# Moving transposes and small gradients in the backward pass of a convolution and joint kernel

## The chip, the cores and the metric

The kernel runs on one core of a Trainium2 chip. The metric is the device time of one execution in microseconds (us). A core has five engines with queues of their own: TensorE (PE, matmuls and transposes into PSUM; PEld is its weight load), VectorE (DVE), ScalarE (ACT), GpSimd (POOL) and SyncE (SP), which issues DMAs here. Engines wait for each other by semaphores, and each works through its queue in order.

## The reference

`x` is (2, 16000, 256), the weights `w1` and `w2` are (3, 256, 256), `g` is (2, 8, 256), and `w_f`, `w_g`, `w_o` are (256, 256), all bf16. The outputs are the forward result and the gradients of all seven inputs.

```python
def conv_half(h, w):                       # 3 taps, padded by 1, then every second row
    hp = jnp.pad(h, ((0,0),(1,1),(0,0)))
    f = sum(jnp.einsum("btc,cd->btd", hp[:, i:i+h.shape[1], :], w[i]) for i in range(3))
    return gelu(f)[:, ::2, :]

f = conv_half(conv_half(x, w1), w2)                        # (2, 4000, 256)
fe, ge = f @ w_f, g @ w_g
j = jnp.tanh(fe[:, :, None, :] + ge[:, None, :, :])        # (2, 4000, 8, 256)
out = jnp.einsum("btud,dv->btuv", j, w_o)
# vjp with grad_out (2, 4000, 8, 256): gradients of x, w1, w2, g, w_f, w_g, w_o
```

## The kernel before, in words

The 4000 rows of each of the two batches are cut into eight chunks of 512 rows (the last has 416), 16 chunks in all, numbered n = 0 to 15. Features lie on the partitions, in two halves of 128; rows lie on the free dimension.

For each chunk the kernel computes, under these names:

- `conv_units`: the first convolution (L246), `HT` after gelu and its derivative `G1`; `conv2_units`: the second one (L279), `FT` and `G2`; `fe_units`: FE = FT times w_f (L302). The gelu is a chain of instructions (`gelu`, L197 and L199): copies of PSUM to `g_x` (L282 in `conv2_units`), the square `g_sq` on ScalarE, `g_s` on VectorE, a sigmoid on ScalarE, and the product (HT or FT) on VectorE; the derivative follows (L199).
- `joint_units`, four times a chunk, each for two of the eight values of u: `gj` computes the square `JSQ` of the tanh (L523), the product of w_o and the transposed gradient (L529), and `NGZ` = (JSQ - 1) times it (L531); `ngfe_acc` sums NGZ over u on GpSimd (L550); `o_block` computes the output (L623, copied out by L625); `gwo` adds to the gradient of w_o in one PSUM tile that lives to the end (L672); `ahead` issues the tanhs of the next pair (L312).
- the backward pass of the chunk before: `d1_units` (GF, L336 and L338), `d5_units` (GH, L366 and L369), `gwf_units` (gradient of w_f, L406), `gw2_units` (rows of HT and GF by transposes on PE, L380, copied by ScalarE, L382, then three groups of w2 products, L437), `e_units`. The last one transposes GH in two groups (L380, copied to `rows` by VectorE, L382), and then goes through the blocks of 128 rows: `gx_block` computes the gradient of x in two halves (L478, copied by L481) and stores it by a DMA on the GpSimd queue (L490); `gw1` computes a group of w1 products (L500), one after each of the first three blocks.

The products of w1, w2 and w_f of a chunk are added to sums in SBUF by `flush` (L320 for the first chunk, L322 after it): ACC1, ACC2, ACCF.

The order of the work: chunk n's joint units are the main line. `weave` takes one piece of the fill (the first convolution of chunk n+1, the backward pass of chunk n-1, the second convolution and FE of n+1) after a piece of the main line, 0.85 pieces on average. The fill's order is written out by hand in the list `parts` (L771 to L787): near its end come the last pieces of w2, `conv2_units`, six pieces of `e_units` (two transposes, four of gx and w1), `fe_units`, and the rest of `e_units`. VectorE's pieces of gelu wait in a queue that `pump` empties. A scheduler then assigns buffers and writes each engine's queue, so that the queues are fixed before the kernel runs. PSUM has one tile for the gradient of w_o and seven that all other results take in turn. JSQ has two buffers, NGZ three, GX two.

After the last chunk comes a tail (L813 to L860): the remaining pieces of w_o's gradient, then `d1`, `d5`, `gwf`, `gw2` and `e` of chunk 15 one after the other, then copies of the sums to bf16 and their stores on SP (L821 to L833), and at the end the gradients of g and w_g: NGGE is the sum over the chunks (L836), and for each batch there are two products with w_g (L845), two transposes (L851), a copy (L853) and two products with g (L855), and at last a copy and a store (L859, L860).

Of the kernel before, what the change touches and what calls it, by code (L numbers as in the profile page):

```python
# [32 lines left out]
def kernel(  # L33
# [279 lines left out]
                                 bias=GE[:, b, mt, u:u + 1], scale=1.0)  # L313


    first_flush = {"1": True, "2": True, "F": True}

    def flush(key, acc, ps):
        if first_flush[key]:
            nc.vector.tensor_copy(out=acc, in_=ps)  # L320
        else:
            nc.vector.tensor_tensor(out=acc, in0=acc, in1=ps, op=ALU.add)  # L322

    def d1_units(n):
        b, ci, c0, W = geom(n)
# [58 lines left out]
    def gwf_units(n):  # L384
        b, ci, c0, W = geom(n)
        st = S[n]
        HT, GF, FT, NG = st["HT"], st["GF"], st["FT"], st["NGFE"]
        bl = blocks(W)
        FN = []
        for k in range(0, len(bl), 2):  # L390
            t = rowp.tile([P, 8, P], BF16, name="rows")
            srcs, dsts = [], []
            for j, (o, M) in enumerate(bl[k:k + 2]):
                for kt in range(KT):
                    srcs.append((FT[:, kt, o:o + M], 4 * j + kt, M))
# [13 lines left out]
        flush("F", ACCF[:], ps[:])  # L409
        first_flush["F"] = False  # L410
        yield

    def gw2_units(n):
        b, ci, c0, W = geom(n)
        st = S[n]
        HT, GF, FT, NG = st["HT"], st["GF"], st["FT"], st["NGFE"]
        bl = blocks(W)
        HG = []
        for (o, M) in bl:
            t = rowp.tile([P, 8, P], BF16, name="rows")  # L420
            srcs = []
            j = 0
            for (par, off) in ((0, 2), (1, 2), (1, 1)):
                for kt in range(KT):
                    srcs.append((HT[:, par, kt, off + o:off + o + M], j, M))
                    j += 1
            for kt in range(KT):
                srcs.append((GF[:, kt, 2 + o:2 + o + M], j, M))
                j += 1
            transposes(srcs, [(t[:M], M, 0, 8)], nc.scalar.copy)  # L430
            HG.append(t)
            yield
        for i, place in ((1, 0), (2, 2), (0, 4)):
            ps = ps_f32()
# [5 lines left out]
            flush("2", ACC2[:, i, :], ps[:])  # L440
            yield
        first_flush["2"] = False
    def e_units(n):
        b, ci, c0, W = geom(n)
        st = S[n]
# [48 lines left out]
        def gw1(i):  # L494
            ps = ps_f32()
            for k, (o, M) in enumerate(bl):
                t, j = GR[k]
                for dt in range(KT):
                    for par in range(2):
                        nc.tensor.matmul(ps[:, dt * D:(dt + 1) * D],  # L500
                                         lhsT=st["X5", o][:M, i + 2 * par, dt * P:(dt + 1) * P],
                                         rhs=t[:M, j + 2 * par:j + 2 * par + 2, :].rearrange("p k d -> p (k d)"),
                                         start=(k == 0 and dt == 0 and par == 0),
                                         stop=(k == len(bl) - 1 and dt == KT - 1 and par == 1))
            flush("1", ACC1[:, i, :], ps[:])
# [6 lines left out]
        first_flush["1"] = False  # L512


    n_gwo = [0]
# [246 lines left out]
    for n in range(G):  # L762
# [3 lines left out]
        if back:  # L766
            for (o, M) in blocks(window(n - 1)[1] - window(n - 1)[0]):
# [16 lines left out]
        if fwd:  # L784
# [5 lines left out]
        for up in range(U // 2):  # L790
# [17 lines left out]
            if up == U // 2 - 1:  # L808
                for _ in fill:
                    pump(2)  # L810
                pump(len(later) + len(lazy))
                lazy_on[0] = False
    n = G - 1  # L813
    gwo_rest(*prev_gwo[0], 0)
    for (o, M) in blocks(window(n)[1] - window(n)[0]):
        load_x5(n, o, M)
    for _ in chain(d1_units(n), d5_units(n), gwf_units(n), gw2_units(n), e_units(n)):
        pass


    for i in range(KK):  # L821
        t_ = gel3.tile([P, 512], BF16, name="g_sq", tag="g_sq")
        nc.scalar.copy(out=t_[:], in_=ACC1[:, i, :])
        nc.sync.dma_start(out=out_2[i].rearrange("(dt p) n -> p dt n", p=P), in_=t_[:].rearrange("p (k n) -> p k n", k=KT))
        t_ = gel3.tile([P, 512], BF16, name="g_s", tag="g_s")
        nc.vector.tensor_copy(out=t_[:], in_=ACC2[:, i, :])
        nc.sync.dma_start(out=out_3[i].rearrange("(dt p) n -> p dt n", p=P), in_=t_[:].rearrange("p (k n) -> p k n", k=KT))
    t_ = gel.tile([P, 512], BF16, name="g_x", tag="g_x")
    nc.vector.tensor_scalar(out=t_[:], in0=ACCF[:], scalar1=-1.0, scalar2=None, op0=ALU.mult)
    nc.sync.dma_start(out=out_5.rearrange("(dt p) n -> p dt n", p=P), in_=t_[:].rearrange("p (k n) -> p k n", k=KT))  # L830
    t_ = gel.tile([P, 512], BF16, name="g_x", tag="g_x")
    nc.scalar.copy(out=t_[:], in_=GWO_ps[:].rearrange("p k v -> p (k v)"))
    nc.sync.dma_start(out=out_7.rearrange("(dt p) n -> p dt n", p=P), in_=t_[:].rearrange("p (k n) -> p k n", k=KT))  # L833

    NGGE = const.tile([P, B, KT, U], FP32, name="NGGE")
    nc.vector.tensor_reduce(out=NGGE[:].rearrange("p b k u -> p (b k u)"),  # L836
                            in_=NGGEc[:].rearrange("p b k u c -> p (b k u) c"),
                            axis=mybir.AxisListType.X, op=ALU.add)
    NGGEb = const.tile([P, B, KT, U], BF16, name="NGGEb")
    nc.vector.tensor_copy(out=NGGEb[:], in_=NGGE[:])  # L840
    GWG_ps = ps_f32()
    for b in range(B):
        gg = ps_f32()
        for kt in range(KT):
            nc.tensor.matmul(gg[:U, 0:D], lhsT=NGGEb[:, b, kt, :], rhs=WGT[:, kt, :], start=(kt == 0), stop=(kt == KT - 1))  # L845
        gg_sb = gxp.tile([U, D], BF16, name="gg_sb")
        nc.scalar.activation(out=gg_sb[:], in_=gg[:U, 0:D], func=ACT.Copy, scale=-1.0)
        nc.sync.dma_start(out=out_4[b], in_=gg_sb[:])
        tr = ps_bf()
        for kt in range(KT):  # L850
            nc.tensor.transpose(out=tr[:U, kt, :], in_=NGGEb[:, b, kt, :], identity=ident[:])  # L851
        ngR = gxp.tile([U, KT, P], BF16, name="ngR")
        nc.vector.tensor_copy(out=ngR[:], in_=tr[:U, 0:KT, :])  # L853
        for dt in range(KT):
            nc.tensor.matmul(GWG_ps[:, dt * D:(dt + 1) * D], lhsT=GR8[:, b, dt * P:(dt + 1) * P],  # L855
                             rhs=ngR[:].rearrange("u kt p -> u (kt p)"),
                             start=(b == 0 and dt == 0), stop=(b == B - 1 and dt == KT - 1))
    t_ = gel3.tile([P, 512], BF16, name="g_sq", tag="g_sq")
    nc.scalar.activation(out=t_[:], in_=GWG_ps[:], func=ACT.Copy, scale=-1.0)  # L859
    nc.sync.dma_start(out=out_6.rearrange("(dt p) n -> p dt n", p=P), in_=t_[:].rearrange("p (k n) -> p k n", k=KT))  # L860


# [1 line left out]
_INS = ['x', 'w1', 'w2', 'g', 'w_f', 'w_g', 'w_o', 'grad_out']  # L864
_OUTS = [((2, 4000, 8, 256), 'bfloat16'), ((2, 16000, 256), 'bfloat16'), ((3, 256, 256), 'bfloat16'), ((3, 256, 256), 'bfloat16'), ((2, 8, 256), 'bfloat16'), ((256, 256), 'bfloat16'), ((256, 256), 'bfloat16'), ((256, 256), 'bfloat16')]
# [25 lines left out]
```

## Time and profile before

| | |
|---|---|
| three runs, median (lowest to highest) | 867.71 us (865.87 to 876.6) |
| the profiled execution | 865.23 us, of which the span is 863.5 us |
| granted clock of TensorE | 0.998 of full speed |
| period of a full chunk (L302 at 573.08 and 625.47 us) | 52.4 us |
| busy share of PE in 100 us to 800 us | 97.6 to 98.8% in each 100 us |
| last 31.5 us | PE busy 25.4 us |

A line of the profile's time line has the start and the duration in us, the engine, the line of the program, the operation, what it writes and reads, and how many instructions were merged; in brackets, the idle time of the engine before it and what ended it. Matmuls overlap, so the time from one start to the next says more than a duration. A line of the list of waits has the engine and what waited, what it waited for, the us in total, how often, and the longest.

### The profile page before, as it was taken

Reading aid. Unit: us, or ns where it says so; the run is one execution under the profiler, and the core shown is the slowest. Engines: PE = TensorE matmul, PEld = TensorE weight load, DVE = VectorE, ACT = ScalarE, POOL = GpSimd, SP = SyncE. Lnnn points to the kernel's source line nnn. Section 1 sums busy time; section 2 is a strip of 40 time slices with the busy share of each in tenths; the row PEclk is TensorE's granted clock in tenths of the full one; section 3 lists DMA queues with packets and bytes.
Section 4 is the critical chain, followed back from the end, with each engine's and each line's share of the span. In section 5 each row is a group of like instructions: output and inputs, shape, how many; then the busy total and the mean of one; then the engine's idle time right before and its main releaser. Section 6 shows DMA issues by size and latency. Waiting matters only on the chain.

```text
span 863.5 us, 17775 instructions
## 1 busy us (share of the span) xinstructions
PE 830.8 (96%) x6648; PEld 598.9 (69%) x6648; DVE 603.8 (70%) x1194; ACT 685.7 (79%) x1067; POOL 410.6 (48%) x457
## 2 busy tenths in 40 slices
PE   8878999999999999999999999999999999999997
PEld 4455776767777677777766677776766867777875
DVE  4797949669495784949578495875949579495553
ACT  4889896986969869696996969788696986969534
POOL 1264553544544544555454455453554544455651
PEclk9999999999999999999999999999999999999999
DMA  9998999999999999999899999999999999999942
GB/s 187 211 215 195 189 250 224 224 243 193 258 206 227 226 217 233 212 227 219 211 203 214 234 215 240 227 210 250 177 263 236 205 211 219 219 243 219 215 140 91
DMA packets 382455, 185.66 MB, mean 215 GB/s; under 512 B 330160, under 2 KB 366280, under 8 KB 382368
## 3 DMA queue, kind: packets, MB, share of 16 engines
q1 hardware_dynamic: 362400, 114.35, 76.4%
q0 software_dynamic: 19968, 70.18, 27.9%
q8 instruction: 52, 0.85, 0.4%
q14 instruction: 35, 0.29, 0.1%
HBM read 54.43 MB, written 50.34 MB: 121 GB/s over the span
## 4 chain that ended last, share of the span: by engine, by line
PE 51%; DVE 30%; ACT 13%; issue 3%; DMA 2%; POOL 0%; ACTq 0%; POOLq 0%; DVEq 0%
PE ps L500 7%; PE ps L246 7%; PE GWO_ps L672 7%; PE ps L529 7%; PE ps L478 7%; PE ps L623 6%; DVE NGZ L531 6%; DVE G L199 5%; DVE g_sq L199 5%; DVE g_s L197 5%; DVE GH L369 3%; ACT JSQ L523 3%; ACT JT L312 3%; PE pst L380 3%; PE ps L366 3%
## 5 line engine op out<-in xcount | busy, mean ns | idle before, releaser
L550 POOL TENSOR_TENSOR ACCN<-ACCN,NGZ 128x1024 f32<-128x1024 f32 (+1 forms) x80 | 170.4, 2130 | 126.5 <-DVE NGZ L531 124.0
L531 DVE SCALAR_TENSOR_TENSOR NGZ<-JSQ,ps 128x512 bf16<-128x512 bf16 (+1 forms) x256 | 163.4, 669 | 83.5 <-ACT GX L481 47.7
L523 ACT ACTIVATE JSQ<-JT 128x1024 bf16<-128x1024 bf16 (+1 forms) x128 | 135.3, 1060 | 86.6 <-DVE NGZ L531 86.6
L312 ACT ACTIVATE JT<-FE,GE 128x512 bf16<-128x512 f32 (+1 forms) x256 | 171.0, 736 | 0.1
L625 ACT CAST OUT<-ps 128x512 bf16<-128x512 f32 x248 | 147.7, 614 | 3.8 <-PE ps L623 3.3
L623 PE MATMUL ps<-WO,JT 128*128 128x256 bf16 x992 | 148.1, 272 | 0.9 <-DVE NGZ L531 0.5
L529 PE MATMUL ps<-GOT,WOT 128*128 128x512 bf16 (+1 forms) x512 | 138.4, 374 | 1.7 <-DVE JR L382 1.1
L672 PE MATMUL GWO_ps<-GO,JR 128*128 128x256 bf16 x992 | 139.7, 273 | 0.0
L197 DVE SCALAR_TENSOR_TENSOR g_s<-g_sq,g_x 128x1024 bf16<-128x1024 bf16 (+1 forms) x45 | 74.6, 1657 | 57.1 <-ACT g_sq L197 57.1
L623 PEld LDWEIGHTS <-JT 128*128 128x128 bf16 x992 | 94.4, 98 | 24.9 <-issue 1.4
L672 PEld LDWEIGHTS <-JR 128*128 128x128 bf16 x992 | 95.1, 98 | 18.2 <-issue 1.1
L322 DVE TENSOR_TENSOR ACC<-ACC,ps 128x512 f32<-128x512 f32 x90 | 59.4, 682 | 66.6 <-PE ps L500 62.0
L478 PE MATMUL ps<-W1T,GH 128*128 128x256 bf16 (+2 forms) x768 | 104.2, 273 | 0.0
L500 PE MATMUL ps<-rows,X 128*128 128x256 bf16 (+2 forms) x768 | 94.2, 272 | 8.2 <-DVE rows L382 8.2
L246 PE MATMUL ps<-XC,W 128*128 128x512 bf16 (+1 forms) x384 | 91.1, 374 | 2.5 <-DMA XC<-in_x_dram 2.1
L500 PEld LDWEIGHTS <-X 128*128 128x128 bf16 (+2 forms) x768 | 74.5, 98 | 23.1 <-issue 11.5
L652 POOL DMA_DIRECT2D out_dram<-OUT x64 | 49.6, 775 | 85.2 <-ACT OUT L625 82.8
L481 ACT CAST GX<-ps 128x512 bf16<-128x512 f32 (+2 forms) x128 | 74.4, 592 | 15.0 <-PE ps L478 7.8
L478 PEld LDWEIGHTS <-GH 128*128 128x128 bf16 (+2 forms) x768 | 75.0, 99 | 15.6 <-issue 1.7
L529 PEld LDWEIGHTS <-WOT 128*128 128x128 bf16 x512 | 49.1, 98 | 43.9 <-issue 2.6
L490 POOL DMA_DIRECT2D out_dram<-GX x64 | 35.9, 560 | 87.3 <-ACT GX L481 81.0
L382 ACT COPY rows<-pst 128x1024 bf16<-128x1024 bf16 x64 | 63.0, 1018 | 9.6 <-PE pst L380 9.5
(139 smaller groups left out, 1264.5 us busy)
## 6 DMA issues: line engine op xcount, KB each, us to landing
GO<-in_grad_out_dram SPq DMA_DIRECT2D x56, 512.0 KB, 5.3
out_dram<-OUT POOLq DMA_DIRECT2D x56, 512.0 KB, 5.6
X<-in_x_dram POOLq DMA_DIRECT2D x58, 320.0 KB, 8.0
out_dram<-GX POOLq DMA_DIRECT2D x58, 256.0 KB, 4.1
JR<-JT SPq DMA_TRANSPOSE x240, 5.1
GO<-in_grad_out_dram SPq DMA_DIRECT2D x8, 384.0 KB, 4.1
out_dram<-OUT POOLq DMA_DIRECT2D x8, 384.0 KB, 4.7
GOT<-in_grad_out_dram SPq DMA_TRANSPOSE x128, 4.6
```

Of the source, the lines that this page charges most:

```text
L197: later.popleft()()
L246: nc.tensor.matmul(ps[:, :W], lhsT=W1[:, i, kt, mt * P:(mt + 1) * P], rhs=st["X", c][:, kt, 16 + sh:16 + sh + W], start=(k == 0), stop=(k ...
L312: nc.scalar.activation(out=JT[:, mt, :W], in_=S[n]["FE"][:, mt, :W], func=ACT.Tanh, bias=GE[:, b, mt, u:u + 1], scale=1.0)
L478: nc.tensor.matmul(ps[:Mx, cj * D:(cj + 1) * D], lhsT=GH[:, par, kt, j:j + Mx], rhs=W1T[:, i, kt, :], start=(k == 0), stop=(k == last))
L500: nc.tensor.matmul(ps[:, dt * D:(dt + 1) * D], lhsT=st["X5", o][:M, i + 2 * par, dt * P:(dt + 1) * P], rhs=t[:M, j + 2 * par:j + 2 * par + ...
L523: nc.scalar.activation(out=JSQ[:, :, :W], in_=JT[:, :, :W], func=ACT.Square)
L529: nc.tensor.matmul(ps[:, :W], lhsT=WOT[:, kt, mt * P:(mt + 1) * P], rhs=GOT[:, kt, :W], start=(kt == 0), stop=(kt == KT - 1))
L531: nc.vector.scalar_tensor_tensor(out=NGZ[:, mt, :W], in0=JSQ[:, mt, :W], scalar=1.0, in1=ps[:, :W], op0=ALU.subtract, op1=ALU.mult, accum_ ...
L550: nc.gpsimd.tensor_tensor(out=out, in0=in0, in1=st["NGZ", u][:, :, :W], op=ALU.add)
L623: nc.tensor.matmul(ps[:M, j * V:(j + 1) * V], lhsT=st["JT", u][:, kt, o:o + M], rhs=WO[:, kt, :], start=(kt == 0), stop=(kt == KT - 1))
L625: nc.scalar.copy(out=OUT[:M, k, :], in_=ps[:M, :])
L672: nc.tensor.matmul(GWO_ps[:, dt, :], lhsT=JR[:M, k, j, dt, :], rhs=GO[:M, k, j * V:(j + 1) * V], start=(n_gwo[0] == 0), stop=(n_gwo[0] == ...
```

## The change

It has four parts. GH's two groups of transposes, the first two pieces of `e_units`, move in the list of the fill from behind `conv2_units` to before the first and before the second group of w2 products, and the pieces of `e_units` between `conv2_units` and `fe_units` are four instead of six. In the last chunk `flush` writes the sum of ACC and PSUM directly to a bf16 tile and stores it. The gradients of w_o, g and w_g become a generator, `small_gradients`, whose pieces stand between those of the last chunk's backward pass. And in the last chunk `e_units` runs the three groups of w1 products first, each followed by a block of gx, and the blocks from the last to the first.

```diff
-    def flush(key, acc, ps):
-        if first_flush[key]:
+    def flush(n, key, i, ps):
+        acc = {"1": ACC1, "2": ACC2}[key][:, i, :] if key != "F" else ACCF[:]
+        if n == G - 1:
+            t = gel3.tile([P, 512], BF16, name="g_sq", tag="g_sq")
+            if key == "F":
+                nc.vector.scalar_tensor_tensor(out=t[:], in0=acc, scalar=-1.0, in1=ps, op0=ALU.mult, op1=ALU.subtract)
+            else:
+                nc.vector.tensor_tensor(out=t[:], in0=acc, in1=ps, op=ALU.add)
+            out = out_5 if key == "F" else {"1": out_2, "2": out_3}[key][i]
+            store_small(out, t)
+        elif n == 0:
             nc.vector.tensor_copy(out=acc, in_=ps)
         else:
             nc.vector.tensor_tensor(out=acc, in0=acc, in1=ps, op=ALU.add)
+    def store_small(out, t):
+        nc.sync.dma_start(out=out.rearrange("(dt p) n -> p dt n", p=P), in_=t[:].rearrange("p (k n) -> p k n", k=KT))
...
+        if n == G - 1:
+            for i in range(KK):
+                gw1(i)
+                yield from gx_block(*bl[-1 - i])
+            yield from gx_block(*bl[0])
+            return
         for k, (o, M) in enumerate(bl):
             yield from gx_block(o, M)
...
-                      islice(d5, 1), islice(gw2, 1), d5, islice(gw2, nhg - 2), gwf, gw2]
+                      islice(d5, 1), islice(gw2, 1), d5, islice(gw2, nhg - 2), gwf, islice(e, 1), islice(gw2, 1),
+                      islice(e, 1), gw2]
...
-            parts.append(islice(e, 6))
+            parts.append(islice(e, 4))
...
+    def small_gradients():
+        t_ = gel.tile([P, 512], BF16, name="g_x", tag="g_x")
+        nc.scalar.copy(out=t_[:], in_=GWO_ps[:].rearrange("p k v -> p (k v)"))
+        store_small(out_7, t_)
...
+        yield
+        GWG_ps = ps_f32()
+        for b in range(B):
+            gg = ps_f32()
+            for kt in range(KT):
+                nc.tensor.matmul(gg[:U, 0:D], lhsT=NGGEb[:, b, kt, :], rhs=WGT[:, kt, :],
+                                 start=(kt == 0), stop=(kt == KT - 1))
...
+            nc.vector.tensor_copy(out=ngR[:], in_=tr[:U, 0:KT, :])
+            yield
+            for dt in range(KT):
+                nc.tensor.matmul(GWG_ps[:, dt * D:(dt + 1) * D], lhsT=GR8[:, b, dt * P:(dt + 1) * P],
...
+        store_small(out_6, t_)
+        yield
...
-    for _ in chain(d1_units(n), d5_units(n), gwf_units(n), gw2_units(n), e_units(n)):
+    small = small_gradients()
+    for _ in chain(d1_units(n), islice(small, 1), d5_units(n), islice(small, 1), gwf_units(n), islice(small, 1),
+                   gw2_units(n), small, e_units(n)):
         pass
-    for i in range(KK):
-        t_ = gel3.tile([P, 512], BF16, name="g_sq", tag="g_sq")
-        nc.scalar.copy(out=t_[:], in_=ACC1[:, i, :])
...
```

More of the change, by code (lines that the diff above doesn't have):

```diff
@@ L313, in tanh @@
                                  bias=GE[:, b, mt, u:u + 1], scale=1.0)
-    first_flush = {"1": True, "2": True, "F": True}
-    def flush(key, acc, ps):
-        if first_flush[key]:
+    def flush(n, key, i, ps):
[9 more added lines that the diff above has]
+        elif n == 0:
             nc.vector.tensor_copy(out=acc, in_=ps)
@@ L408, in gwf_units @@
                                  start=(k == 0 and dt == 0), stop=(k == len(FN) - 1 and dt == KT - 1))
-        flush("F", ACCF[:], ps[:])
-        first_flush["F"] = False
+        flush(n, "F", 0, ps[:])
         yield
@@ L439, in gw2_units @@
                                      start=(k == 0 and dt == 0), stop=(k == len(bl) - 1 and dt == KT - 1))
-            flush("2", ACC2[:, i, :], ps[:])
+            flush(n, "2", i, ps[:])
             yield
-        first_flush["2"] = False
     def e_units(n):
@@ L504, in gw1 @@
                                          stop=(k == len(bl) - 1 and dt == KT - 1 and par == 1))
-            flush("1", ACC1[:, i, :], ps[:])
+            flush(n, "1", i, ps[:])
+        if n == G - 1:
[4 more added lines that the diff above has]
+            return
         for k, (o, M) in enumerate(bl):
@@ L511, in e_units @@
                 yield
-        first_flush["1"] = False
     n_gwo = [0]
@@ L812 @@
                 lazy_on[0] = False
+    def small_gradients():
+        t_ = gel.tile([P, 512], BF16, name="g_x", tag="g_x")
+        nc.scalar.copy(out=t_[:], in_=GWO_ps[:].rearrange("p k v -> p (k v)"))
+        store_small(out_7, t_)
+        NGGE = const.tile([P, B, KT, U], FP32, name="NGGE")
+        nc.vector.tensor_reduce(out=NGGE[:].rearrange("p b k u -> p (b k u)"),
+                                in_=NGGEc[:].rearrange("p b k u c -> p (b k u) c"),
+                                axis=mybir.AxisListType.X, op=ALU.add)
+        NGGEb = const.tile([P, B, KT, U], BF16, name="NGGEb")
+        nc.vector.tensor_copy(out=NGGEb[:], in_=NGGE[:])
+        yield
[5 more added lines that the diff above has]
+                                 start=(kt == 0), stop=(kt == KT - 1))
+            gg_sb = gxp.tile([U, D], BF16, name="gg_sb")
+            nc.scalar.activation(out=gg_sb[:], in_=gg[:U, 0:D], func=ACT.Copy, scale=-1.0)
+            nc.sync.dma_start(out=out_4[b], in_=gg_sb[:])
+            tr = ps_bf()
+            for kt in range(KT):
+                nc.tensor.transpose(out=tr[:U, kt, :], in_=NGGEb[:, b, kt, :], identity=ident[:])
+            ngR = gxp.tile([U, KT, P], BF16, name="ngR")
+            nc.vector.tensor_copy(out=ngR[:], in_=tr[:U, 0:KT, :])
+            yield
+            for dt in range(KT):
+                nc.tensor.matmul(GWG_ps[:, dt * D:(dt + 1) * D], lhsT=GR8[:, b, dt * P:(dt + 1) * P],
+                                 rhs=ngR[:].rearrange("u kt p -> u (kt p)"),
+                                 start=(b == 0 and dt == 0), stop=(b == B - 1 and dt == KT - 1))
+        t_ = gel.tile([P, 512], BF16, name="g_x", tag="g_x")
+        nc.scalar.activation(out=t_[:], in_=GWG_ps[:], func=ACT.Copy, scale=-1.0)
+        store_small(out_6, t_)
+        yield
     n = G - 1
@@ L816 @@
         load_x5(n, o, M)
-    for _ in chain(d1_units(n), d5_units(n), gwf_units(n), gw2_units(n), e_units(n)):
-        pass
-    for i in range(KK):
-        t_ = gel3.tile([P, 512], BF16, name="g_sq", tag="g_sq")
-        nc.scalar.copy(out=t_[:], in_=ACC1[:, i, :])
[L824 to L857, printed above, removed]
@@ L858 @@
-    t_ = gel3.tile([P, 512], BF16, name="g_sq", tag="g_sq")
-    nc.scalar.activation(out=t_[:], in_=GWG_ps[:], func=ACT.Copy, scale=-1.0)
-    nc.sync.dma_start(out=out_6.rearrange("(dt p) n -> p dt n", p=P), in_=t_[:].rearrange("p (k n) -> p k n", k=KT))
+    small = small_gradients()
+    for _ in chain(d1_units(n), islice(small, 1), d5_units(n), islice(small, 1), gwf_units(n), islice(small, 1),
+                   gw2_units(n), small, e_units(n)):
+        pass
 _INS = ['x', 'w1', 'w2', 'g', 'w_f', 'w_g', 'w_o', 'grad_out']
```

## The prediction

> **What bounds the kernel now.** I read the page's busy shares first, then the list of what TensorE (PE) waited for, then the time lines of the four engines around one place, then the end of the chain.
>
> ```profile
> PE 830.8 (96%) x6648; PEld 598.9 (69%) x6648; DVE 603.8 (70%) x1194; ACT 685.7 (79%) x1067; POOL 410.6 (48%) x457
> ```
> PE is the bound: 32.7 us of the 863.5 us span are not PE; by the table of stretches 13.4 of them lie in the first 88 us, 6.1 in the last 31.5, 13 between. The change adds no matmul and takes none away, so it can only close or open holes on PE, and move what comes after PE's last matmul. The holes are these:
>
> ```profile
> PE ps L500 <- DVE rows L382: 8.2, 12, 0.8
> PE pst L380 <- DVE GH L369: 3.8, 11, 0.5
> ```
> The first is what the change aims at: the w1 products wait 12 times for the copy of GH's transposed rows. One full chunk (the eleventh, n=10) shows it, and what comes behind it on PE:
>
> ```profile
> 570.24 1.03 PE L500 MATMUL ps<-rows,X 128*128 128x256 bf16 x8 [0.83 <-DVE rows L382]
> ...
> 573.08 1.03 PE L302 MATMUL ps<-FT,WF 128*128 128x512 bf16 x4
> ```
> L302 needs FT, the end of the gelu chain of the next chunk's second convolution: g_x copies (ACT), g_sq (ACT), g_s (DVE), sigmoid (ACT), FT (DVE). VectorE's and ScalarE's rows of it, with GpSimd's beside:
>
> ```profile
> 546.59 1.23 DVE L197 SCALAR_TENSOR_TENSOR g_s<-g_sq,g_x 128x1024 bf16<-128x1024 bf16 x1 [0.62 <-ACT g_sq L197]
> ...
> 562.73 0.68 DVE L531 SCALAR_TENSOR_TENSOR NGZ<-JSQ,ps 128x512 bf16<-128x512 bf16 x1
> ...
> 567.25 2.34 DVE L197 SCALAR_TENSOR_TENSOR g_s<-g_sq,g_x 128x1024 bf16<-128x1024 bf16 x1 [1.41 <-ACT g_sq L197]
> ```
> ```profile
> 564.11 1.06 ACT L523 ACTIVATE JSQ<-JT 128x1024 bf16<-128x1024 bf16 x1 [5.95 <-DVE NGZ L531]
> 565.07 1.05 ACT L282 CAST g_x<-ps 128x512 bf16<-128x512 f32 x2
> 566.16 1.06 ACT L197 ACTIVATE g_sq<-g_x 128x1024 bf16<-128x1024 bf16 x1
> 567.12 0.57 ACT L625 CAST OUT<-ps 128x512 bf16<-128x512 f32 x1
> 567.59 1.06 ACT L523 ACTIVATE JSQ<-JT 128x1024 bf16<-128x1024 bf16 x1
> ```
> ```profile
> 564.17 4.34 POOL L550 TENSOR_TENSOR ACCN<-ACCN,NGZ 128x1024 f32<-128x1024 f32 x2 [2.90 <-DVE NGZ L531]
> ```
> To see: a JSQ waits until the second NGZ before it has freed its buffer. g_x and g_sq stand behind one JSQ; the second JSQ comes after g_sq. FT ends at 571.40, so L302 has 1.68 us to spare. The tail:
>
> ```profile
> 845.44 1.42 PE ps L478 x12
> 846.86 1.85 PE ps L500 x16
> ...
> 859.04 0.60 ACT g_sq L859
> ```
> The end is a chain of small gradients behind the last GX block: 2.36 us from 856.66 to 859.02, then an ACT copy. Of the output stores, the block stores of GX on the GpSimd queue, then the last one on SP, took from issue to landing:
>
> ```profile
> DMA to landing us min/median/max: 2.0/2.4/2.7
> ```
> ```profile
> DMA to landing us min/median/max: 1.8/1.8/1.8
> ```
>
> **The change part by part: the chunks.** The work of 14 chunks (1 to 14) is affected. In the compiled order of the changed kernel GH's two transpose groups (8 of 0.055 us) stand before and after the first group of w2 products, the other two groups stand between the L529s, and both L279 groups move behind all L529s, next to two L623s. L302 stays where it was.
>
> On PE alone, from 556.42: transposes 0.45, L672 0.44, L437 0.87, transposes 0.45, and so on. The 0.83 us wait of L500 goes, and about 0.18 us that L437 waited for ACT's rows (weight loads waited 2.5 us over nine places). What is late next are PSUM buffers, seven taken in turn. The second L437 takes the one that ACCF frees at 559.80 (wanted 559.49: 0.3 to 0.4 us); the third takes the one that GH's first rows copy frees at 561.62 (wanted 561.16: 0.5 us). So PE could reach L302 between 571.9 (no buffer late) and 572.8, against 573.08: the gain is at most 1.17 us a chunk.
>
> The FT chain is the other arm. VectorE is back to back until 560.93 in either kernel. From there, by 0.605 us a slot (NGZ 562.73, 563.33): rows, ACC, rows, NGZ at 562.74, NGZ 563.35, ACC, NGZ, ACC, fourth NGZ at 565.77. On ACT the compiled order is now JSQ, JSQ, g_x, OUT, g_x, OUT, g_sq, GX, GX, sigmoid: both JSQs stand ahead of the g_x copies. This is the wait that the change adds. The second JSQ starts 0.78 us after the fourth NGZ starts (as 564.11 follows 563.33), at 566.55. Behind it are queued g_x at 567.51, OUT 567.99, g_x 568.47, OUT 568.95 (0.48 apart, as 567.12 to 567.59), g_sq 569.43 to 570.49. Then g_s on VectorE: 1.23 us (row at 546.59) or 2.34 us (row at 567.25). The second overlaps GpSimd's adds, which end at 568.51, and ends 1.08 us after them; the first meets none. Now GpSimd's second add starts after the fourth NGZ and ends at about 568.7, before g_s, so I take 1.23 and keep 2.34 as the upper end. g_s 570.52 to 571.75, sigmoid 571.78 to 572.84, FT 572.87 to 573.56, L302 at 573.60. That is later than PE's own arrival, so it sets the time: 0.52 us later than before, with all of PE queued behind it. From the first NGZ to L302 it is 10.87 us.
>
> After L302 the order is as before, and the next chunk's late points (the 3.8 us at L380) are anchored to PE, so the delay is passed on.
>
> The trace shows g_s stretched beside GpSimd's add and not beside idle GpSimd. The Trainium skill, "SBUF — State Buffer", section "Who interferes with whom", says that a VectorE instruction with two SBUF inputs and a GpSimd instruction that reads SBUF exclude each other for the whole instruction. By that rule g_s costs 1.23 us here as long as the add has ended, and the trace agrees (2.34 with 1.26 us of overlap).
>
> Sum over the chunks: n=2 to 5 and 10 to 13 are alike, 8 x 0.52 = 4.2. For the others I put 10.87 us behind their first NGZ (0.2 more where a short last block makes three rows copies): n=8 457.95 gives 469.0 against 468.62, +0.4; n=9 510.59 gives 521.7 against 520.68, +1.0; n=1 has one 0.6 us multiply moved behind the NGZs, 108.5 against 108.13, +0.4; n=7 has shorter rows (416 columns), about +0.8; n=6 and 14, whose chain of 416 columns is some 0.8 shorter, -0.1 each. Together **+6.6 us**.
>
> No DMA of a chunk is moved but one GOT load that changes place with a JR transpose on SP, and two tiny G1h copies on GpSimd that now stand behind two adds (4.3 us) in two chunks; their readers are one chunk later. If that cover were gone they would cost those 4.3 us once.
>
> **The tail.** (a) The last sums go from PSUM straight to bf16 tiles: three ACT copies of 0.62 and four VectorE copies of 0.43 vanish; all lay beside PE matmuls, nothing gained on the path. The new sums to bf16 have no row; the nearest are ACC (0.69) and NGZ (0.68, bf16 out), so 0.69, as the adds they replace. Eleven small stores on SP come earlier or in another order; only stores are behind them. (b) The small gradients move up. Their first matmuls (0.43) fill the hole before L406 (838.11), but the 0.28 ngR copy stands before the rows copies on VectorE: L406 at 838.37. The second set (0.43) and the four products (0.39 a pair) stand before the HT transposes, and two ACT copies (0.37) before the rows copies on ACT: rows from 840.7 instead of 839.85, L437 done at 845.3 instead of 844.44, GH's transposes at 846.4 (845.44). (c) L478 no longer stands between these and the first L500. The rows copies wait behind three sums on VectorE and end first at 847.4: a hole of 1.0 us that 1.42 us of L478 used to cover. From 847.42: three L500 of 1.85 and the L478 of four blocks, 1.42 each, that is 5.55 + 5.68: PE ends at 858.65, only 0.37 us before the old 859.02. (d) Behind it: GX copy to 859.44, 0.30 until GpSimd issues (before: 847.48 to 847.78), 2.4 landing: 862.1. Before: ACT ends 859.64, SP issues 859.67, 1.8 landing: 861.5. The tail: **+0.7 us**; bounds -1.3 (no hole, no delay of rows: old PE end 856.66 before the small gradients, 857.45, 857.75, 860.15) to +1.5 (landing 2.7, and 0.5 more at rows).
>
> Sum: the profiled execution took 865.23 us (span 863.5 and 1.7 around it); +6.6 +0.7 = **872.5 us**. The median of the three runs is 867.71, 0.3% above that execution, so 872.5 is 0.6% above the median.
>
> **The rivals.**
> 1. *L302 does not wait.* If ACT got to g_x sooner, PE's arrival would set the time: at most 0.28 us gained in 8 chunks (2.2), little in the rest, tail +0.7: **863.7**. For it: the margin of the chain over PE's arrival is 0.8 us. Against it: every gap in the chain was taken from a row.
> 2. *The change does what it says.* All of L500's 8.2 us and L437's 2.5 us go, nothing else waits, the tail's lower bound -1.3 holds: **853.2**. It needs FT 1.7 us earlier than I have it.
> 3. *g_s meets GpSimd's add* (slower than before). If the second add starts after 568.4 instead of 566.6, its 2.17 us reach beyond 570.52 and g_s takes up to 2.34: 1.11 us more in 12 chunks, 13.3: **885.8**. For it: so it is in 12 chunks now. Against it: 1.8 us of distance.
>
> **How the numbers follow.** Forecast 0.62, rival 1 0.20, rival 2 0.06, rival 3 0.12. Predicted 872.5. The range 861 to 882 holds the forecast, rival 1 and the lower half-way cases of rival 3; left out are rival 2 and most of rival 3, under 0.2. A measurement of this kernel can tell about 2% (17 us: under 850.4, over 885.1). Faster by over 2% needs rival 2 and more: 0.02. Slower by over 2% is half of rival 3: 0.06. The rest, 0.92, is within 2%; the forecast's own range, 868 to 877, is inside it.
>
> **What would show it.** In the profile after: L500's wait for rows gone from the list of PE's waits, and a wait of L302 for FT, about 0.8 us a chunk, in its place; ACT's second JSQ idle before it for NGZ, g_x behind it; g_s at 1.23 us. In the tail a hole of 1 us before the first L500, and the last store on the GpSimd queue. Wrong: no L302 in that list (rival 1), g_s at 2.3 us (rival 3), or PE's last matmul before 857.

## The result, and the profile after

| | before | after |
|---|---|---|
| median of 22 runs each (lowest to highest) | 867.84 us (865.77 to 887.69) | 874.73 us (871.72 to 878.18) |
| ratio of after to before, 95% interval | | 1.0063 (1.0043 to 1.0083) |
| the profiled execution, and its span | 865.23 us, 863.5 us | 876.07 us, 874.3 us |

The changed kernel is slower by 0.6%, less than the 2% that count as a difference here; the prediction was 872.5 us and "within 2%". Ratios and their intervals, here and below, compare the fast executions alone, so they are not the quotients of the medians. The two profiled executions are 10.8 us apart. Cut at the instruction that the prediction followed, the first L302 of each chunk, the difference lies here:

| stretch | before | after | difference |
|---|---|---|---|
| start to the second L302 (no changed code) | 63.04 | 64.88 | +1.84 |
| eight full chunks (n=2 to 5, 10 to 13), each | 52.39 | 52.91 | +0.52 |
| n=12, beyond that | | | +1.45 |
| n = 1, 6, 7, 8, 9, 14 | | | +0.25, +0.19, +0.25, -0.05, +0.86, +0.10 |
| last L302 to the end of the span | 83.09 | 84.81 | +1.72 |

The first row and n=12 are chance of one execution: none of the four other kernels with this chunk order below (chunk_only, last_on_sp, gx_first, two_on_sp) shows such a chunk n=12, and the start lies between 61.7 and 66.6 us in all profiles whatever the kernel. What the change itself did is 5.8 us in the chunks (8 x 0.52 and the six others) and 1.7 in the tail. Line numbers of the changed program: L437 is now L447, L380 L391, L382 L393, L500 L510, L478 L488, L490 (GX's store) L500, L523 L538, L531 L546, L320 and L322 (`flush`) L328 and L330, L550 L565, L625 L640, L529 L544, L623 L638, L672 L687, L406 L417, L366 and L369 (GH) L377 and L380.

PE's share, and its waits, from the page and the list of waits of the changed kernel:

```profile
PE 827.3 (95%) x6574; PEld 600.0 (69%) x6648; DVE 582.7 (67%) x1190; ACT 682.4 (78%) x1064; POOL 410.3 (47%) x457
```
```profile
PE ps L302 <- DVE FT L197: 9.7, 11, 3.0
...
PE ps L447 <- DVE rows L393: 3.1, 9, 0.3
...
PE ps L447 <- DVE ACCF L330: 2.3, 10, 0.3
...
PE ps L510 <- DVE rows L393: 0.9, 1, 0.9
```

In the kernel before, L302 waited for FT only once, at the start:

```profile
PE ps L302 <- DVE FT L197: 3.0, 1, 3.0
```
The wait of the w1 products for their rows, 8.2 us before, is down to one of 0.9 (the tail). In its place L302 waits for FT, 6.7 us more than before, and L447 waits for two PSUM buffers. The profile has only 6574 of the 6648 matmuls, so PE's busy time is a little low here. The same full chunk as in the prediction, PE first:

```profile
565.31 1.03 PE L447 MATMUL ps<-rows 128*128 128x256 bf16 x8 [0.21 <-DVE ACCF L330]
566.18 0.59 PE L544 MATMUL ps<-GOT,WOT 128*128 128x512 bf16 x2
567.12 1.03 PE L447 MATMUL ps<-rows 128*128 128x256 bf16 x8 [0.34 <-DVE rows L393]
...
574.52 1.91 PE L510 MATMUL ps<-rows,X 128*128 128x256 bf16 x16
...
577.79 0.60 PE L687 MATMUL GWO_ps<-GO,JR 128*128 128x256 bf16 x4
579.05 1.02 PE L302 MATMUL ps<-FT,WF 128*128 128x512 bf16 x3 [0.66 <-DVE FT L197]
```
The w1 products run without a gap (no bracket), but 4.5 us later L302 stands 0.66 us. The brackets count from the end of the matmul ahead; from start to start the waits are longer. The four L687 start 0.109 us apart, so L302 could have started at 578.23 and lost 0.82 us; the two waits of L447 are 0.37 and 0.51 us in the same way. What FT waited for, on ScalarE, VectorE and GpSimd:

```profile
569.56 1.06 ACT L538 ACTIVATE JSQ<-JT 128x1024 bf16<-128x1024 bf16 x1 [5.95 <-DVE NGZ L546]
571.98 1.06 ACT L538 ACTIVATE JSQ<-JT 128x1024 bf16<-128x1024 bf16 x1 [1.35 <-DVE NGZ L546]
572.94 0.57 ACT L282 CAST g_x<-ps 128x512 bf16<-128x512 f32 x1
...
574.84 1.09 ACT L197 ACTIVATE g_sq<-g_x 128x1024 bf16<-128x1024 bf16 x1
```
```profile
575.96 1.23 DVE L197 SCALAR_TENSOR_TENSOR g_s<-g_sq,g_x 128x1024 bf16<-128x1024 bf16 x1 [4.08 <-ACT g_sq L197]
...
578.31 0.69 DVE L197 TENSOR_TENSOR FT<-g_s,g_x 128x1024 bf16<-128x1024 bf16 x1 [0.66 <-ACT g_s L197]
```
```profile
572.03 2.13 POOL L565 TENSOR_TENSOR ACCN<-ACCN,NGZ 128x1024 f32<-128x1024 f32 x1 [0.28 <-DVE NGZ L546]
```
To see: two JSQs follow each other, the second stands 1.35 us for its buffer, and g_x waits behind it though its matmuls are long done. GpSimd's add ends at 574.16, 1.8 us before g_s, which takes 1.23 us and not 2.34. The tail, on PE, ScalarE and GpSimd:

```profile
856.53 2.01 PE L510 MATMUL ps<-rows,X 128*128 128x256 bf16 x16 [0.92 <-DVE rows L393]
```
```profile
865.11 2.79 PE L488 MATMUL ps<-W1T,GH 128*128 128x256 bf16 x24
```
```profile
866.02 2.51 ACT L491 CAST GX<-ps 128x512 bf16<-128x512 f32 x4 [2.07 <-PE ps L488]
```
```profile
868.82 0.54 POOL L500 DMA_DIRECT2D out_dram<-GX  x1 [0.76 <-ACT GX L491]
```
To see: the hole of 0.92 us before the first w1 product, PE's last matmul, and GX's last store on the GpSimd queue. It lands 2.3 us after its start, at 871.1, and the span ends at 874.3.

### The profile page after: what moved, and what is told of

It is laid out like the page before. It is cut to its first block, busy times and chain, and to the rows that moved or that the text cites. A ratio compares the mean times of both kernels' runs of the same rounds, so it can differ in the third digit from the quotient of the medians.

```text
span 874.3 us, 17713 instructions
## 1 busy us (share of the span) xinstructions
PE 827.3 (95%) x6574; PEld 600.0 (69%) x6648; DVE 582.7 (67%) x1190; ACT 682.4 (78%) x1064; POOL 410.3 (47%) x457
## 4 chain that ended last, share of the span: by engine, by line
ACT 33%; DVE 29%; PE 22%; issue 10%; DMA 3%; POOL 1%; ACTq 0%; POOLq 0%; DVEq 0%
ACT JT L312 10%; DVE NGZ L546 7%; ACT OUT L640 5%; DVE G L199 5%; DVE g_sq L199 5%; ACT JSQ L538 4%; ACT g_sq L197 4%; DVE GH L380 4%; ACT GX L491 4%; DVE g_s L197 4%; PE GWO_ps L687 3%; PE ps L638 3%; PE ps L544 2%; ACT g_x L249 2%; PE ps L510 2%
## 5 line engine op out<-in xcount | busy, mean ns | idle before, releaser
L565 POOL TENSOR_TENSOR ACCN<-ACCN,NGZ 128x1024 f32<-128x1024 f32 (+1 forms) x80 | 170.9, 2137 | 142.4 <-DVE NGZ L546 141.0
L538 ACT ACTIVATE JSQ<-JT 128x1024 bf16<-128x1024 bf16 (+1 forms) x128 | 135.1, 1059 | 113.6 <-DVE NGZ L546 113.6
L546 DVE SCALAR_TENSOR_TENSOR NGZ<-JSQ,ps 128x512 bf16<-128x512 bf16 (+1 forms) x256 | 164.0, 669 | 77.7 <-ACT GX L491 40.6
L640 ACT CAST OUT<-ps 128x512 bf16<-128x512 f32 x248 | 146.6, 613 | 3.6 <-PE ps L638 3.5
L638 PE MATMUL ps<-WO,JT 128*128 128x256 bf16 x992 | 148.1, 272 | 1.4 <-DVE NGZ L546 0.5
L687 PE MATMUL GWO_ps<-GO,JR 128*128 128x256 bf16 x992 | 140.1, 273 | 0.0
L544 PE MATMUL ps<-GOT,WOT 128*128 128x512 bf16 (+1 forms) x472 | 134.5, 373 | 4.7 <-DVE JR L393 1.3
L197 DVE SCALAR_TENSOR_TENSOR g_s<-g_sq,g_x 128x1024 bf16<-128x1024 bf16 (+1 forms) x45 | 57.6, 1280 | 95.3 <-ACT g_sq L197 95.3
L638 PEld LDWEIGHTS <-JT 128*128 128x128 bf16 x992 | 95.6, 98 | 31.1 <-issue 1.4
L687 PEld LDWEIGHTS <-JR 128*128 128x128 bf16 x992 | 94.8, 98 | 17.9 <-issue 1.1
L488 PE MATMUL ps<-W1T,GH 128*128 128x256 bf16 (+2 forms) x768 | 104.0, 273 | 0.0
L510 PE MATMUL ps<-rows,X 128*128 128x256 bf16 (+2 forms) x768 | 92.3, 273 | 0.9 <-DVE rows L393 0.9
L246 PE MATMUL ps<-XC,W 128*128 128x512 bf16 (+1 forms) x370 | 88.9, 375 | 3.3 <-DMA XC<-in_x_dram 2.6
L330 DVE TENSOR_TENSOR ACC<-ACC,ps 128x512 f32<-128x512 f32 x84 | 57.3, 683 | 47.0 <-PE ps L510 46.9
L488 PEld LDWEIGHTS <-GH 128*128 128x128 bf16 (+2 forms) x768 | 75.1, 99 | 15.2 <-issue 1.1
L510 PEld LDWEIGHTS <-X 128*128 128x128 bf16 (+2 forms) x768 | 74.5, 98 | 14.1 <-issue 2.4
L544 PEld LDWEIGHTS <-WOT 128*128 128x128 bf16 x512 | 48.5, 98 | 39.5 <-issue 4.1
L500 POOL DMA_DIRECT2D out_dram<-GX x64 | 35.8, 560 | 68.1 <-ACT GX L491 64.3
L246 PEld LDWEIGHTS <-W 128*128 128x128 bf16 x384 | 37.6, 98 | 40.6 <-issue 4.1
```

The lines of the kernel that those rows point to most:

```text
L197: later.popleft()()
L246: nc.tensor.matmul(ps[:, :W], lhsT=W1[:, i, kt, mt * P:(mt + 1) * P], rhs=st["X", c][:, kt, 16 + sh:16 + sh + W], start=(k == 0), stop=(k ...
L488: nc.tensor.matmul(ps[:Mx, cj * D:(cj + 1) * D], lhsT=GH[:, par, kt, j:j + Mx], rhs=W1T[:, i, kt, :], start=(k == 0), stop=(k == last))
L510: nc.tensor.matmul(ps[:, dt * D:(dt + 1) * D], lhsT=st["X5", o][:M, i + 2 * par, dt * P:(dt + 1) * P], rhs=t[:M, j + 2 * par:j + 2 * par + ...
L538: nc.scalar.activation(out=JSQ[:, :, :W], in_=JT[:, :, :W], func=ACT.Square)
L544: nc.tensor.matmul(ps[:, :W], lhsT=WOT[:, kt, mt * P:(mt + 1) * P], rhs=GOT[:, kt, :W], start=(kt == 0), stop=(kt == KT - 1))
```

## The experiments

Two theories were to be told apart for the chunks: the second JSQ, with the gelu chain of FT queued behind it, sets the time of L302 (theory); the PSUM buffers that the moved transposes take set it (rival). For the tail: which of its terms is the missing us. The kernels marked (a) ran on one chip beside 33 runs of the kernel before (median 867.08 us), those marked (b) beside 17 (868.05), those marked (c) beside 23 (870.13). A difference of one profile alone is read from its time line, chunk by chunk. "Tail" is the time from the last L302 to the end of the span.

**The two halves alone (a).** tail_only has the chunk order of the kernel before and the changed tail:

```diff
-                      islice(d5, 1), islice(gw2, 1), d5, islice(gw2, nhg - 2), gwf, islice(e, 1), islice(gw2, 1),
-                      islice(e, 1), gw2]
+                      islice(d5, 1), islice(gw2, 1), d5, islice(gw2, nhg - 2), gwf, gw2]
...
-            parts.append(islice(e, 4))
+            parts.append(islice(e, 6))
```

> The changed tail with the chunk order of the kernel before. Theory (the chunks lose by ScalarE's order, the tail loses by itself): period of a full chunk 52.40 us as before, the tail 1.7 us longer, so about 869.5 us, ratio 1.002. Rival (the tail gains what the small gradients took off the end, and the chunks lose more than I think): about 865 us, ratio 0.997.

Measured: 868.63 us, ratio 1.002 (0.9989 to 1.0051); periods of 52.40, tail 84.81. Its list of PE's waits has the wait of the w1 products again, and L302 only once, at the start:

```profile
PE ps L510 <- DVE rows L393: 9.1, 13, 0.9
...
PE ps L302 <- DVE FT L197: 3.0, 1, 3.0
```

chunk_only is the opposite: the kernel before, with only the two pieces of `e_units` moved.

```diff
-                      islice(d5, 1), islice(gw2, 1), d5, islice(gw2, nhg - 2), gwf, gw2]
+                      islice(d5, 1), islice(gw2, 1), d5, islice(gw2, nhg - 2), gwf, islice(e, 1), islice(gw2, 1),
+                      islice(e, 1), gw2]
...
-            parts.append(islice(e, 6))
+            parts.append(islice(e, 4))
```

> The changed chunk order with the tail of the kernel before. Theory: period 52.92 us, L302 waits 0.66 us for FT in each full chunk, 5.8 us more over the chunks, the tail as before: about 873.6 us, ratio 1.0067. Rival (the tail makes the difference): about 868 us, ratio 1.000.

Measured: 873.95 us, ratio 1.0078 (1.0055 to 1.0102); periods of 52.92, tail 83.04 against 83.09 before. L302's 9.7 us are there, and not those of the w1 products. So the loss is in the chunk order, and the tail adds 1.7 us that the times of tail_only alone cannot tell from nothing.

**The order that keeps g_x ahead of the second JSQ (a).** In conv2_first the second convolution comes before the last two groups of w2 products:

```diff
-                      islice(e, 1), gw2]
+                      islice(e, 1)]
...
             parts.append(conv2_units(n + 1))
         if back:
-            parts.append(islice(e, 4))
+            parts += [gw2, islice(e, 4)]
```

> The changed kernel, but the second convolution stands ahead of the last two groups of w2 products, GH's transposes where the change puts them. Theory (the loss is g_x behind two JSQs on ScalarE): g_x stands behind one JSQ again, L302 doesn't wait, L500 doesn't wait either, period about 51.6 us, some 8 us less over the chunks, tail +1.7: about 861.5 us, ratio 0.993. Rival (the loss is PSUM buffers that come free late, 0.5 us a chunk before L437): those waits stay, period 52.1 to 52.4, about 867 us, ratio 0.999.

Measured: 867.93 us, ratio 1.0021 (0.9988 to 1.0055); period 52.14; tail 84.83. The theory's 51.6 did not come, and 52.14 lies in the rival's range. L302 waits no more in the chunks, and comes 0.73 us earlier after the last unmoved L638 than in the kernel before; but 0.5 us is taken back by new waits for PSUM buffers:

```profile
PE ps L302 <- DVE FT L197: 3.0, 1, 3.0
PE ps L488 <- DVE ACC L330: 3.0, 9, 0.4
...
PE ps L279 <- DVE ACCF L330: 2.3, 10, 0.3
```
L488 behind L302 takes the buffer that the first w1 sum frees, and that sum now stands behind the pieces of the gelu's derivative on VectorE. So the wait of L302 goes when g_x is ahead of the JSQ, as the theory has it; its size was missed, because the buffers that the rival speaks of come next.

**A third JSQ buffer (a).** jsq3 leaves the order and takes the second JSQ's wait away; to make room, the tiles of the incoming gradient go from six to five.

```diff
-    gotp = pool("gotp", 6)
+    gotp = pool("gotp", 5)
...
-    jsp = pool("jsp", 2)
+    jsp = pool("jsp", 3)
```

> The changed kernel with three buffers for JSQ instead of two (and five for GOT instead of six, to make room). Theory: the JSQ ahead of g_x waits for the second NGZ and not the fourth, g_x starts 2.4 us sooner, L302 no longer waits for FT, period about 52.1 us, set by PE and the two waits for PSUM; g_s now meets GpSimd's second add and takes about 1.7 us instead of 1.23 us, hidden. About 867 us, ratio 0.999. Rival (PSUM buffers): period stays 52.9, about 874.5 us, ratio 1.007.

Measured: 868.67 us, ratio 1.0017 (0.9993 to 1.0041); period 52.41, where 52.1 was expected. L302's waits are gone but for the one at the start:

```profile
PE ps L544 <- DMA GOT<-in_grad_out_dram: 5.4, 2, 5.2
PE ps L302 <- DVE FT L197: 3.0, 1, 3.0
...
PE ps L447 <- DVE rows L393: 2.7, 8, 0.3
PE ps L377 <- DVE GH L380: 2.2, 9, 0.6
```
The first line is one late load, which made one chunk 58.7 us long in this execution. It may be the price of five tiles, but that is not shown: best1 below, with six, has a chunk of 58.98 us in which PE waits for another load. The execution's time is thus no clean measure; six of its eight full chunks take 52.41 or 52.42 us. In them L302 comes 16.79 us after the last unmoved L638, where it was 17.10 in the kernel before. That 0.31 us of gain is lost again 28 us later, where the products of L377 wait for VectorE's GH (last line; they start 0.3 us later after L302 than in the kernel before).

**One unit of conv2 between the last two w2 groups (b).** conv2_mid puts one g_x between the two JSQs:

```diff
-                      islice(e, 1), gw2]
+                      islice(e, 1), islice(gw2, 1)]
...
-            parts.append(islice(e, 4))
+            parts += [gw2, islice(e, 4)]
```

> The changed kernel, with one conv2 unit between the third and the fourth block of w2 products, so that ScalarE has one g_x between its two JSQ copies. Theory (the second JSQ stands 1.35 us for the fourth NGZ and everything behind it comes late): the g_x (about 0.47 us and its OUT) runs inside that wait, FT ends 0.5 to 0.9 us earlier against the L302 before, its 0.66 us wait in a full chunk is gone, and the period falls from 52.91 to about 52.4, where the PSUM waits of the L447 blocks leave it. Rival (the FT wait is only the last of several, and the PSUM buffers set the time): L302 waits for FT no more or less than 0.3, but the period stays at 52.8 to 52.9.

Measured: 867.38 us in one run; period 52.08, tail 84.81. L302 waits for FT in no full chunk. ScalarE in the same chunk:

```profile
565.65 1.06 ACT L538 ACTIVATE JSQ<-JT 128x1024 bf16<-128x1024 bf16 x1 [5.96 <-DVE NGZ L546]
566.61 0.57 ACT L282 CAST g_x<-ps 128x512 bf16<-128x512 f32 x1
567.46 1.06 ACT L538 ACTIVATE JSQ<-JT 128x1024 bf16<-128x1024 bf16 x1 [0.28 <-DVE NGZ L546]
568.42 0.57 ACT L282 CAST g_x<-ps 128x512 bf16<-128x512 f32 x1
568.89 0.59 ACT L640 CAST OUT<-ps 128x512 bf16<-128x512 f32 x1
569.37 1.07 ACT L197 ACTIVATE g_sq<-g_x 128x1024 bf16<-128x1024 bf16 x1
```
The first g_x fills the wait, only 0.28 us of it is left, and g_sq starts 3.72 us after the first JSQ instead of 5.28. The PSUM waits are as in the changed kernel (3.1 and 2.3 us in the list, the first now at L279), GH's transposes are where the change put them, and yet a chunk takes 0.83 us less than in the changed kernel and 0.31 less than before. This decides between the two: the wait behind the second JSQ is the loss, and the PSUM buffers set the time only once it is gone. It is better than the theory's 52.4.

**The end of the tail (b).** last_on_sp issues GX's very last store from SyncE:

```diff
-            nc.gpsimd.dma_start(out=ap4, in_=t[p0:M].rearrange("p f d -> p (f d)"))
+            last = n == G - 1 and o == 0
+            (nc.sync if last else nc.gpsimd).dma_start(out=ap4, in_=t[p0:M].rearrange("p f d -> p (f d)"))
```

> The changed kernel, with the very last GX store issued by SyncE in place of GpSimd; nothing else moves. In the profile of the changed kernel the span goes on for 3.2 us after the last landing, against 2.0 in the kernel before, whose last store is the same one from the same queue. Theory (the extra comes from something else than that queue, for instance from which transfers are still out): issue lag 0.03 in place of 0.30 and a landing of about 1.9 in place of 2.3, so about 0.7 us less from the end of the last GX copy to the landing, and 3.2 us after it still: copy end to span end 14.9 - 0.7 = about 5 us or more. Rival (the end of the GpSimd queue is what takes the extra us): 2.0 us after the landing, 1.9 us less in all. The chunks stay at periods of 52.9.

(The 14.9 in that text is a slip: in the changed kernel the last GX copy ends at 868.53 and the span at 874.3, 5.8 us later, and 5.8 - 0.7 is the 5 us that it goes on with.) Measured: 874.84 us in one run; copy end to span end 4.4 us (868.67 to 873.1), between the two. The 2.0 us of the kernel before, from which the rival starts, follow the landing of a small store of SyncE and not of the same GX store. PE lost 1.5 us by chance in this tail (its sixteen L510 took 3.5 us instead of 2.0), so its length, 85.05, is no measure. GpSimd's last store, now the last but one, starts at 867.65, 5.45 us before the end. That suggested a rule: the span ends some 5.5 us after the start of the last store that GpSimd issues, whatever else there is. It holds in every profile to that point but one:

| kernel | last GpSimd store starts, us before the end | last SyncE store starts, us before the end |
|---|---|---|
| before | 5.55 | 3.83 |
| after | 5.48 | 8.4 |
| tail_only, conv2_first, jsq3, gx_first, conv2_mid | 5.44 to 5.50 | 7 and more |
| chunk_only | 5.50 | 3.79 |
| last_on_sp | 5.45 | 4.41 |
| best1 | 6.47 | 3.04 |

(The page gives the span in tenths of a us, so the hundredths here are good to 0.05.) The kernel before fits the rule, too: its end was set by a GX store of GpSimd and not, as I had it, by the last store on SyncE, at 859.67:

```profile
857.95 0.56 POOL L490 DMA_DIRECT2D out_dram<-GX  x1 [0.49 <-ACT gg_sb L847]
```
The trace also has what lies between that store and the end. GpSimd's queue ends with a DRAIN, an instruction that the busy shares and the page's chain leave out; the kernel before, then the changed one (count; shortest, median and longest duration in ns; first and last start in us):

```profile
L886 POOLq DRAIN  x3: 46/103/4743, 857.9 to 863.2; - x3
```
```profile
L895 POOLq DRAIN  x3: 46/103/4722, 868.8 to 874.0; - x3
```
The long one starts with the last store (857.93 and 868.80) and ends at 862.67 and 873.52; the 0.8 us to the end of the span are semaphores and short DRAINs of all engines. It takes 4.60 to 4.74 us in all 13 profiles, so 4.7 and 0.8 make the 5.5. In best1 it is over 1.8 us before the end, and GpSimd then waits for SyncE, whose last store lands later.

**Two stores on SyncE (c).** two_on_sp tests the rule, by taking the last two stores off GpSimd:

```diff
-            nc.gpsimd.dma_start(out=ap4, in_=t[p0:M].rearrange("p f d -> p (f d)"))
+            late = n == G - 1 and o in (bl[0][0], bl[1][0])
+            (nc.sync if late else nc.gpsimd).dma_start(out=ap4, in_=t[p0:M].rearrange("p f d -> p (f d)"))
```

> The changed kernel, with the last two GX stores issued by SyncE in place of GpSimd. In ten profiles so far the span ended 5.44 to 5.55 us after the start of the last store that GpSimd issued, whatever its size and whatever came later on SyncE (one exception, with a SyncE store 3.4 us later, ended 3.04 us after that one). Theory (the end of the span is the later of the last GpSimd store's start + 5.5 and the last SyncE store's start + 3.0 to 3.8): counted from the last L302, GpSimd's last store now starts at about 74.8, which gives 80.3; SyncE's starts at 79.1, which gives 82.1 to 82.9, against 84.8 in the changed kernel: 1.9 to 2.7 us less, and under 3.0 us between the last landing and the end less the rest. Rival (the end follows the last matmul or copy, and which queue stores is all the same): 84.0 to 84.8; with the last store alone on SyncE the span ended 5.06 us after the last matmul, which would be 83.5 here.

Measured: 869.94 us in one run; tail 82.02 us against 84.81, 2.8 us less; PE ends as in the changed kernel, 78.41 us after the last L302. GpSimd's last store starts 7.3 us before the end, and SyncE's two like this (L501 is this kernel's line of the store):

```profile
863.93 1.66 SPq L501 DMA_DIRECT2D out_dram<-GX  x2
```
The second of the two starts at 865.24 by the rows of that line (0.35 us each), 2.96 us before the end. The tail is 0.1 us below the theory's 82.1 to 82.9; the rival's 83.5 or more is out. A store of 256 KB lands 2.3 us after its start on the GpSimd queue and 2.0 on SyncE's, so that the span goes on for 3.2 us after the one and 1.0 us after the other.

**The hole before the w1 products (b).** gx_first puts a gx block ahead of each group of w1 products in the last chunk:

```diff
             for i in range(KK):
-                gw1(i)
                 yield from gx_block(*bl[-1 - i])
+                gw1(i)
```

> The changed kernel, with the GX block of the last chunk ahead of each group of w1 products again, as in the kernel before. Theory: the 0.92 us that the first w1 product of the tail waits for the copied rows is gone, since eight matmuls on W1T and GH (8 x 116 ns = about 0.9 us or more) stand between the row transposes and the first w1 product; the end of PE comes 0.9 us earlier against the last L302, and with it the last store, if the last GX copy still follows directly on the last matmul. Rival: the wait is only moved, because the w1 block after the last GX block lies last and its sums and stores (ACC add, output tile, landing) come later than the GX copy did: PE ends 0.9 us earlier, but the last landing comes 0 to 1 us later than in the changed kernel. The chunks stay at 52.9.

Measured: 875.42 us in one run; tail 83.70 against 84.81. PE, behind GH's transposes at 854.85:

```profile
855.86 1.47 PE L488 MATMUL ps<-W1T,GH 128*34 128x256 bf16 x12
857.27 2.02 PE L510 MATMUL ps<-rows,X 128*128 128x256 bf16 x16
```
L488 covers the copy and L510 has no wait; PE ends 1.07 us earlier (77.34 after the last L302), and so does GpSimd's last store. The rival's loss at the end does not come.

**Put together.** best1 (b) and best2 (c) have conv2_first's order and gx_first's and last_on_sp's tail; best1 also moves the small gradients in between the last gx blocks. best3 (c) is best2 with conv2_mid's order.

```diff
-    for _ in chain(d1_units(n), islice(small, 1), d5_units(n), islice(small, 1), gwf_units(n), islice(small, 1),
-                   gw2_units(n), small, e_units(n)):
+    e = e_units(n)
+    for _ in chain(d1_units(n), islice(small, 1), d5_units(n), gwf_units(n), gw2_units(n), islice(e, 4), islice(small, 1),
+                   islice(e, 2), islice(small, 1), islice(e, 2), small, e):
```

> The changed kernel with the second conv2 block ahead of the last two blocks of w2 products, and a tail in which the GX blocks go first, the small gradients lie among the last chunk's units and the last store is issued by SyncE. Theory (the FT chain behind the second JSQ costs the chunks, and the tail has 0.9 us of hole and a landing that can be shortened): period 52.14 as it was with conv2 first, 0.25 x 8 = 2.0 us less than the kernel before in the chunks, and 0 to 2 us less in the tail: 863 to 866, ratio 0.996 to 0.998. Rival (the gain in the chunks is given back by the PSUM waits of L488 and L279, and the tail has no more to give): 867 to 868, ratio 1.000 to 1.002.

> The changed kernel with conv2 ahead of the last two blocks of w2 products (as in conv2_first), the GX blocks ahead of the w1 products in the last chunk (as in gx_first) and the last GX store on SyncE (as in last_on_sp). Theory (each of the three acts where it was measured): the stretch from the first to the last L302 is 715.6 against 717.4 in the kernel before, the tail behind the last L302 about 81.0 (last GX copy at 78.0 + 3.0, while GpSimd's last store at 75.0 + 5.5 is earlier) against 83.1: 3.9 us less than the kernel before, 864 us, ratio 0.9955. Rival (the gains were chance of single profiles, and the small gradients that end the w1 products now end last): ratio 0.998 to 1.0.

> As best2, but with conv2 between the third and the fourth block of w2 products (as in conv2_mid). Theory: period 52.08 again, 0.31 x 8 = 2.5 us less than before in the full chunks, of which some 1.5 are given back in the short ones (n = 1, 8 and 9, as in the profile of conv2_mid), and the same tail of 81.0 in place of 83.1: 3 us less than the kernel before, 865 us, ratio 0.9965, equal to best2 or up to 1 us above. Rival: the tail is the same but conv2_mid's longer chunk of 53.3 was chance, and then it is as good as best2 or better by 0.5 us: 863.5.

| kernel | median | ratio to before (95%) | period | tail |
|---|---|---|---|---|
| best1 | 865.86 us | 0.9961 (0.9938 to 0.9983) | 52.17 | 81.64 |
| best2 | 865.17 us | 0.9935 (0.9898 to 0.9973) | 52.17 | 80.99 |
| best3 | 866.41 us | 0.9937 (0.9903 to 0.9972) | 52.09 | 81.03 |

All three are faster than the kernel before, by 0.4 to 0.65%, and than the changed one. The tails of best2 and best3 came out as the rule gives (81.0); best2's stretch from the second to the last L302 (the 715.6 and 717.4 of the expectation are of this stretch, too) was 717.2 us, and n=8 alone took 1.2 us of that. Between best2 and best3 the runs do not decide; in single profiles the chunk n=8 varies between 51.7 and 53.6 us in kernels of every order, which hides half a us.

## Why the prediction was right, and what was mis-sized

The likeliest case came true. By its steps:

- *"L302 at 573.60 ... 0.52 us later than before"*: each full chunk is 0.52 us longer, and L302 comes 10.87 us after the first NGZ, as worked out. The second JSQ's wait, the g_x behind it and the g_s of 1.23 us are as written; jsq3 and conv2_mid, which take that wait away in two ways, end L302's wait in the full chunks.
- *PE's own arrival*: estimated 0.28 to 1.17 us earlier than before; without the JSQ wait it is 0.30 (conv2_mid 52.08, jsq3's 16.79 against 17.10), so the lower end was right, and both PSUM waits came as sized (0.37 and 0.51 us from start to start, where 0.3 to 0.4 and 0.5 were predicted). The margin of the chain over it is 0.81 us (from the same L687 to L302 it is 18.04 us in the changed kernel and 17.23 in conv2_mid); 0.8 was predicted. Rival 1 is thus what conv2_mid does, with the gain that rival 1 gave.
- *The other chunks*: 5.8 us came for 6.6. The 10.87 us of a full chunk were put behind the first NGZ there without a row of such a chunk. For n=1 and 9 that held (10.88). But in n=6, 7, 8 and 14 L302 does not wait for FT in the changed kernel, and comes 9.75 to 10.61 us after the first NGZ: n=7 gave 0.25 us instead of 0.8, n=8 nothing instead of 0.4 (less than that chunk varies between profiles), and n=6 and 14 gave 0.19 and 0.10 where 0.1 less each was predicted. What sets the time in these four was not followed.
- *Rival 3*: the add ends 1.8 us before g_s, the distance that spoke against it.
- *Tail, (a) to (d)*: rows, L417, the hole (0.92 for 1.0), PE's end and the issue of the last store are within 0.1 us (858.65, 859.75 when the 9.07 us of the later last L302 are taken off).
- *The step that failed*: "Before: ACT ends 859.64, SP issues 859.67, 1.8 landing: 861.5. The tail: +0.7 us". I compared the landings of two stores of different queues, as if the span ended equally long after either. The profile before had two ends within 0.8 us, and the one that set the time was GpSimd's store at 857.95; it moves by 1.79 us (77.54 to 79.33 after the last L302), and the tail by 1.72. The page shows both stores, and its chain ends with ScalarE's copy at L859; the trace had GpSimd's DRAIN, and the runs in which a store was moved confirm it.

The two errors (-0.8 and +1.0) cancel nearly, which is luck: 7.5 us by the profiles, 6.9 by the medians and 5.5 (3.7 to 7.2) by the ratio, where 7.3 was predicted. The time itself, 872.5 us, came out 2.2 us too low because the sum starts from one execution, of 865.23 us, and the median of 22 is 867.84.

That g_s is slower beside GpSimd's add shows in three durations: 1.23 us with the add 1.8 us away, 2.34 with 1.26 us of overlap, and in jsq3 1.52:

```profile
626.43 1.52 DVE L197 SCALAR_TENSOR_TENSOR g_s<-g_sq,g_x 128x1024 bf16<-128x1024 bf16 x1 [1.84 <-ACT g_sq L197]
```
```profile
624.74 2.13 POOL L565 TENSOR_TENSOR ACCN<-ACCN,NGZ 128x1024 f32<-128x1024 f32 x1 [0.28 <-DVE NGZ L546]
```
The add ends at 626.87, and g_s 1.08 us later, exactly as in the kernel before. In the three profiles (before, changed, jsq3) all 31 g_s of this shape that overlap an add already running, by over 0.3 us, end 1.08 to 1.09 us after it. The Trainium skill, "SBUF — State Buffer", section "Who interferes with whom", says that a VectorE instruction with two SBUF inputs contends with a GpSimd instruction that reads SBUF, and calls the port pair that they share an exclusive lock; these rows agree.

## What to carry to other kernels

When a wait on the bounding engine is removed, follow the queue of the other engines to the next thing that this engine needs: here the move that freed PE from a wait of 0.83 us also put two waiting instructions ahead of the chain that PE needs 4.5 us later, and one unit between them gave the gain back. Where two instructions ahead of a chain on a busy engine wait for the same pair of buffers, try a piece of the chain that is ready between them; here that was worth 0.83 us a chunk. At the end of a kernel, compare not when the last data land but, per queue, when the last store is issued and what the span takes after it.

## What was not expected of the hardware

The end of the span comes 5.44 to 5.55 us after the start of the last store on the GpSimd queue (9 profiles, stores of 66 KB and of 256 KB alike), or 2.96 to 3.05 us after the start of the last one on SyncE (best1, best2, best3, two_on_sp), whichever is later. GpSimd's store itself lands after 2.0 to 2.3 us. What runs beyond that is the DRAIN on GpSimd's queue, 4.60 to 4.74 us long whether the store before it lands after 2.0 us or after 2.3; why it takes that long no run shows, and that stays open. Taking the last two GX stores of a tail off that queue gained 2.8 us.
